# Another order of issue for a kernel of attention and two expert blocks

## The chip, the cores and the metric

The kernel runs on one core of one Trainium2 chip. The metric is the time of one execution on the device in microseconds (us); below it the span is the time from the first to the last instruction of the profiled execution. TensorE is called PE in the rows, VectorE DVE, ScalarE ACT, GpSimd POOL and SyncE SP.

## The reference

Shapes: q, k, v are 4 x 12 x 448 x 64 (batch, head, sequence, dimension); the model width is 768.

```python
q_n, k_n = rmsnorm(q, g_q), rmsnorm(k, g_k)
attn = softmax(q_n @ k_n.T / 8)                 # rows divided by sum + 1e-9
x = (attn @ v), heads joined                    # 4 x 448 x 768

h = relu(x @ w_in)                              # moe: 768 -> 1024
u, v = h[..., :512], h[..., 512:]
v_n = (v - mean) / sqrt(var + 1e-6)
v_s = einsum('ts,bsd->btd', w_spatial, v_n) + b_spatial
x = (u * v_s) @ w_out                           # 512 -> 768

xn = (x - mean) / sqrt(var + 1e-6) * g_ln       # moe2
out = x + relu(xn @ w_ch1) @ w_ch2              # 768 -> 3072 -> 768
```

## The kernel before, in words

All products are taken in fp16 with a high and a low half (a value x becomes fp16(x) and fp16(x - fp16(x))), so a product is three matmuls. A copy on ACT makes the high half, a subtraction on VectorE the low half.

The program has three stages. **Attention** works on 24 pairs of heads. `att_load` fetches q, k (tile `raw`) and v (`vraw`); `att_front` takes squares on ACT (L179) and their sums on VectorE (L180); `att_back` multiplies by the inverse norm (L200), writes the high half on ACT (L202) and the low half (L203, on VectorE for pair 0 and on GpSimd for the others), transposes by DMA (L206) and copies the k halves to the other partitions by two more DMAs (L208). `s_mm` makes scores (L240), `softmax1` takes the negative maximum (L251) and the exp (L256), and `av_mm` multiplies by v. `v_scale` reduces v for its scale: for batch 0 on VectorE (L145), for the others as squares with a sum on ACT (L143). Weights come in a wide format and are unpacked by three VectorE instructions each (L419, L420, L421).

**moe1** runs once for each of four batches and is merged with the attention of the next ones. Its banks are `psv`, `psu`, `pss` and `pso`: L590 makes the v half, L612 the u half (its maximum is taken by L616), L630 and L632 the spatial product (`pss`), which L634 multiplies into u as soon as the scale from the maxima is there, L635 and L636 split the result, and L649 and L659 are the output product, stored to `x2d` in DRAM.

**ffn** is the second expert block. `layernorm` loads `x2d` (`lv`), takes statistics (L680, L681), splits (L695 on ACT, L693 on VectorE), makes the sums of a fast 2 x 2 product (L701 to L704), and transposes by DMA (L697) into `xnT`. It works on half 0 (batches 0 and 1) and half 1. `prep_w1` brings in weights of one of twelve blocks (L535 and L536 split them) and `prep_w2` the second weights (L396). `ffn1` makes seven products in four banks ps1x, ps1y, ps1z and ps1w (L728), combines them on VectorE (L735: tq, tu, td, tc, tb) and splits the hidden values (L740, L741, L759, L760); `ffn2` multiplies (L779) and adds into the output (L783). Attention's memory pool is released before the layernorm's is allocated.

The program above is only the list of work. At its end `issue_order` rearranges it: it makes a graph of all instructions with a cost and a latency for each, and `schedule` goes through it, always issuing the instruction that can start first and, at a tie, the one with the smaller priority number. The priorities come from alternating passes backward and forward. `SHAKES` is a table of triples (seed, spread, passes): in each, a seeded generator picks a stretch of the priorities and shakes them by up to the spread, then the passes run. What comes out is one fixed order for each engine's queue, SP's included (SP issues nearly all DMAs), and each engine runs its queue in that order.

Of the kernel before, what the change touches and what calls it, by code (L numbers as in the profile page):

```python
# [795 lines left out]
def weave(a, b):  # L796

    out = [iter(a), iter(b)]
    while out:
        for g in list(out):  # L800
# [10 lines left out]
WINDOW = 3413  # L811


SHAKES = ((0, 0, 6), (1368, 300, 1), (577, 8000, 1), (1518, 3000, 1), (439, 1000, 1), (1820, 40000, 3), (267, 8000,
          1), (505, 300, 3), (827, 8000, 1), (1565, 8000, 3), (426, 20000, 2), (1065, 20000, 1), (1830, 1000, 3),
          (631, 1000, 1), (625, 40000, 2))


def free_size(ap):
# [225 lines left out]
def issue_order(tc):  # L1045
# [3 lines left out]
    prio = [float(o.n) for o in g.ops]  # L1049
    for seed, spread, passes in SHAKES:  # L1050
        rnd = random.Random(seed)
# [203 lines left out]
```

## Time and profile before

| | us |
|---|---|
| median of 3 runs | 1148.35 |
| lowest, highest | 1147.45, 1148.98 |
| the profiled execution's own time | 1147.53 |
| its span | 1145.7 |
| TensorE busy (93% of the span) | 1060.9 |
| VectorE busy (81%) | 930.2 |
| ACT busy (51%) | 585.3 |
| GpSimd busy (23%) | 267.0 |

A row of a timeline gives an instruction's start and duration; in square brackets behind it stands how long its engine sat idle before it and which instruction or DMA ended that. Busy time is where an engine has an instruction at work; an engine that is busy over the whole of a stretch sets that stretch's length. The granted clock is TensorE's, 1.00 being 2.4 GHz.

### The profile page before, as it was taken

What the parts mean: (1) busy time and instruction counts of PE and PEld (TensorE: products, weight loads), DVE (VectorE), ACT (ScalarE), POOL (GpSimd) and SP (SyncE); (2) the same over time, 40 slices, a digit from 0 to 9 for tenths busy, and PEclk for the clock granted to TensorE, in tenths of its full rate; (3) what the DMA queues carried; (4) which work ended last, traced back from release to release, by engine and by line L of the source; (5) the groups of instructions that cost most, each with busy time, mean ns of one, the idle gap of its engine ahead of it and who ended that gap; (6) DMA issues with size and microseconds to landing.
All of it is one profiled execution on the core that took longest, in us unless ns stands there. A gap on an engine that the chain in (4) does not pass through costs nothing.

```text
span 1145.7 us, 16730 instructions
## 1 busy us (share of the span) xinstructions
PE 1060.9 (93%) x6256; PEld 553.8 (48%) x6256; DVE 930.2 (81%) x1629; ACT 585.3 (51%) x1134; POOL 267.0 (23%) x187
## 2 busy tenths in 40 slices
PE   0699999899999999987799999999999999999998
PEld 0344344444444545343455555555555555555554
DVE  7899999859986987979978878686888888686445
ACT  2799987778876855556332414243243334142110
POOL 3462564366345211113010101011011011010000
PEclk9999999999999999998899999999999999999999
DMA  7988899789898976779752220211122221200013
GB/s 222 275 222 221 181 195 175 154 225 191 155 195 187 186 165 190 149 181 243 151 163 88 78 84 28 83 55 57 57 81 84 83 68 49 78 28 1 1 42 152
DMA packets 229457, 149.56 MB, mean 131 GB/s; under 512 B 190272, under 2 KB 206592, under 8 KB 229376
## 3 DMA queue, kind: packets, MB, share of 16 engines
q1 hardware_dynamic: 224992, 137.49, 50.3%
q10 hardware_dynamic: 4384, 11.01, 3.1%
q8 instruction: 49, 0.80, 0.3%
q14 instruction: 32, 0.26, 0.1%
HBM read 86.30 MB, written 11.01 MB: 85 GB/s over the span
## 4 chain that ended last, share of the span: by engine, by line
PE 50%; DVE 4%; POOL 0%; issue 0%; ACT 0%; DVEq 0%
PE ps L779 27%; PE ps1x L728 6%; PE ps1z L728 6%; PE ps1w L728 6%; PE ps1y L728 3%; DVE x L783 1%; DVE x L693 1%; DVE w1v L536 0%; POOL rsr_x L566 0%; DVE lst L680 0%; DVE r_f L420 0%; ACT x L695 0%; DVE h L741 0%; DVE lv L704 0%; DVE lv L703 0%
## 5 line engine op out<-in xcount | busy, mean ns | idle before, releaser
L779 PE MATMUL ps<-w,h 128*128 128x384 f16 x2016 | 388.1, 330 | 10.8 <-ACT h L740 3.8
L779 PEld LDWEIGHTS <-h 128*128 128x128 f16 x2016 | 198.4, 99 | 161.0 <-issue 13.2
L783 DVE SCALAR_TENSOR_TENSOR x<-ps,wio,x 128x768 f32<-128x768 f32 x168 | 169.6, 1014 | 82.9 <-PE ps L779 81.7
L728 PEld LDWEIGHTS <-w1v 128*128 128x128 f16 x1512 | 147.4, 98 | 129.0 <-issue 5.7
L240 PE MATMUL ps_s<-hT 128*64 128x448 f16 x672 | 102.5, 374 | 41.7 <-DMA hT<-qk 28.5
L256 ACT ACTIVATE pexp<-ps_s,nb 128x448 f32<-128x448 f32 x168 | 108.4, 666 | 29.3 <-DVE nb L251 26.6
L527 POOL TENSOR_TENSOR sums<-r_f 128x384 f32<-128x384 f32 x12 | 14.4, 1199 | 427.7 <-ACT r_f L524 340.5
L728 PE MATMUL ps1x<-xnT,w1v 128*128 128x448 f16 x432 | 110.0, 353 | 0.0
L728 PE MATMUL ps1w<-xnT,w1v 128*128 128x448 f16 x432 | 105.8, 352 | 0.0
L728 PE MATMUL ps1z<-xnT,w1v 128*128 128x448 f16 x432 | 104.6, 352 | 0.0
L251 DVE TENSOR_REDUCE nb<-ps_s 128x2 f32<-128x896 f32 x96 | 91.5, 963 | 12.9 <-PE ps_s L240 12.5
L240 PEld LDWEIGHTS <-hT 128*64 128x64 f16 x672 | 39.0, 111 | 89.3 <-issue 42.0
L203 POOL TENSOR_TENSOR qk<-raw,qk 128x896 f16<-128x896 f32 x23 | 47.4, 2062 | 85.5 <-ACT qk L202 58.9
L590 PE MATMUL psv<-w_v,xT 128*128 128x512 f16 (+1 forms) x360 | 63.1, 343 | 2.5 <-ACT vr L594 2.5
L276 DVE SCALAR_TENSOR_TENSOR p<-pexp,p 128x896 f16<-128x896 f32 (+1 forms) x60 | 64.2, 1071 | 1.4 <-ACT p L275 1.0
L740 ACT ACTIVATE h<-td 128x448 f16<-128x448 f32 x24 | 13.8, 576 | 96.7 <-DVE td L735 96.6
L612 PE MATMUL psu<-xT,w_u 128*128 128x448 f16 x288 | 61.7, 354 | 0.3 <-ACT u L615 0.2
L185 POOL TENSOR_TENSOR rs<-ss,mhalf 128x28 f32<-128x28 f32 (+1 forms) x12 | 57.7, 4810 | 15.0 <-DVE ss L182 7.1
L728 PE MATMUL ps1y<-xnT,w1v 128*128 128x448 f16 x216 | 55.1, 353 | 2.8 <-DMA xnT<-x 2.8
L275 ACT ACTIVATE p<-pexp 128x896 f16<-128x896 f32 (+1 forms) x60 | 51.5, 873 | 1.0 <-DMA pT<-p 0.8
L649 PE MATMUL pso<-w_o,g 128*128 128x384 f16 x288 | 51.3, 327 | 0.7 <-DVE u L634 0.7
L748 ACT ACTIVATE tp<-ps1x 128x448 f32<-128x448 f32 x24 | 12.9, 538 | 76.0 <-PE ps1x L728 76.0
(229 smaller groups left out, 1724.6 us busy)
## 6 DMA issues: line engine op xcount, KB each, us to landing
r_w<-in_moe_w_ch_dram SPq DMA_DIRECT2D x48, 768.0 KB, 4.4
raw<-in_q_dram SPq DMA_DIRECT2D x24, 224.0 KB, 3.9
raw<-in_k_dram SPq DMA_DIRECT2D x24, 224.0 KB, 4.2
vpre<-in_v_dram SPq DMA_DIRECT2D x12, 448.0 KB, 4.6
vraw<-in_v_dram SPq DMA_DIRECT2D x24, 224.0 KB, 4.4
hT<-hT SPq DMA_DIRECT2D x48, 112.0 KB, 3.2
lv<-x2d SPq DMA_DIRECT2D x16, 336.0 KB, 5.1
x<-x2d ACTq DMA_DIRECT2D x14, 384.0 KB, 4.6
```

Source lines behind the costliest of these rows:

```text
L185: nc.gpsimd.tensor_tensor(rs, ss, c.mhalf[:, 0:14 * m], op=ALU.pow)
L240: nc.tensor.matmul(ps[hd * 64:hd * 64 + 64, :S], p.hT[:, blk, hd * 64:hd * 64 + 64], kt[:, :, hd * 64:hd * 64 + 64], start=(t == 0), stop= ...
L251: nc.vector.tensor_reduce(nb[:, 0:n], ps[:, 0:n, :S], axis=AX.X, op=ALU.max, negate=True)
L256: nc.scalar.activation(pe[:, j, :], ps[:, j, :S], AF.Exp, bias=nb[:, j:j + 1], scale=1.0, accum_out=p.sm[:, blk:blk + 1])
L275: nc.scalar.activation(p16[:, 0:n, 0], x, AF.Copy, scale=2.0 ** 14)
L276: nc.vector.scalar_tensor_tensor(p16[:, 0:n, 1], x, 2.0 ** 14, p16[:, 0:n, 0], op0=ALU.mult, op1=ALU.subtract)
L590: nc.tensor.matmul(ps[m * h:m * h + m, 0:hn], xT[:, k, x, t * P:t * P + m], wv[:, w, k, h * hn:(h + 1) * hn], start=(n == 0), stop=(n == l ...
L612: nc.tensor.matmul(ps[:, :S], wu[:, w, k, f * P:(f + 1) * P], xT[:, k, x, :], start=(n == 0), stop=(n == len(mms) - 1))
L649: nc.tensor.matmul(ps[:, 0:384], g16[:, f, g, s0:s0 + m], wo[:, w, f, e * 384:(e + 1) * 384], start=(n == 0), stop=(n == len(mms) - 1))
L728: nc.tensor.matmul(ps, w[:, a, x, d], xnT[:, :, 21 * y + 3 * b + d], start=first and n == 0, stop=n == 8, skip_group_check=True)
L779: nc.tensor.matmul(ps[:, e, 0:QK], h16[:, f, x, t * P:(t + 1) * P], w2[:, y, f, e * QK:(e + 1) * QK], start=n == 0, stop=n == 5)
L783: nc.vector.scalar_tensor_tensor(x2, ps[:, :, 0:QK], io[:, 0:1], x2, op0=ALU.mult, op1=ALU.add)
```

## The change

The table `SHAKES` is replaced by another of the same length. Nothing else differs: the same instructions, in another order on every engine. In the words of the change, the order was picked by its mean time when replayed with shaken durations and clock phases.

```diff
-SHAKES = ((0, 0, 6), (1368, 300, 1), (577, 8000, 1), (1518, 3000, 1), (439, 1000, 1), (1820, 40000, 3), (267, 8000,
...
+SHAKES = ((0, 0, 2), (217, 40000, 1), (1364, 300, 1), (1883, 20000, 1), (170, 20000, 1), (261, 8000, 3), (807, 8000,
...
```

What this moves is shown at three places. Behind an arrow stand the operands, then the size.

**The start, VectorE.** This is the end of the operand for pair 0 (raw_111 is its q and k, qk_0 the fp16 result; v_w and v_f are a raw and an unpacked weight, vpre a part of v, raw_165 pair 1). Before:

```order
L200 TENSOR_TENSOR raw_111<-raw_111,rs_143 128x896
L419 TENSOR_SCALAR v_f<-v_w_290 128x512
L420 SCALAR_TENSOR_TENSOR v_f<-v_w_290,v_f 128x512
L203 TENSOR_TENSOR qk_0_158<-raw_111,qk_0_158 128x14x64
L421 SCALAR_TENSOR_TENSOR v_f<-v_w_290,v_f 128x512
```

Now:

```order
L421 SCALAR_TENSOR_TENSOR v_f<-v_w_290,v_f 128x512
L145 TENSOR_REDUCE vparts_190<-vpre_0_191 128x1
L189 TENSOR_SCALAR rs_143<-rs_143,qa 128x7
L200 TENSOR_TENSOR raw_111<-raw_111,rs_143 128x896
L145 TENSOR_REDUCE vparts_190<-vpre_1_194 128x1
L200 TENSOR_TENSOR raw_165<-raw_165,rs_187 128x896
L203 TENSOR_TENSOR qk_0_158<-raw_111,qk_0_158 128x14x64
```

L421, two L145 and the L200 of pair 1 stand ahead of L203 now. On ACT, the last L143 and the L179 of pair 3 stand ahead of the first L256 instead of behind it, and on SP the two copies L208 of pair 0 follow each other.

**The crossing from moe1 of batch 3 to ffn, VectorE and SP.** On VectorE, the rows from the split of the first `pss` bank to that of the last (u is the gated value, g its fp16 halves, lmv and x_0 belong to the layernorm of half 0, w1v, r_0 and r_1 to weights). Before:

```order
L636 TENSOR_TENSOR g_3_5584<-u_5397,g_3_5584 128x448
L634 SCALAR_TENSOR_TENSOR u_5397<-pss_1_5601,isp_5582,u_5397 128x448
L683 TENSOR_SCALAR lmv_3_0_5504<-lmv_3_0_5504,rsr_x_3_0_5510 112x1
L683 TENSOR_SCALAR lmv_3_1_5516<-lmv_3_1_5516,rsr_x_3_1_5522 112x1
L522 TENSOR_SCALAR wgs_5138<-gln,wsc_0_5135 128x6
L621 TENSOR_TENSOR io_5580<-wsc_g_5577,wsc_o 128x1
L636 TENSOR_TENSOR g_3_5584<-u_5397,g_3_5584 128x448
L634 SCALAR_TENSOR_TENSOR u_5397<-pss_2_5617,isp_5582,u_5397 128x448
L636 TENSOR_TENSOR g_3_5584<-u_5397,g_3_5584 128x448
L634 SCALAR_TENSOR_TENSOR u_5397<-pss_3_5644,isp_5582,u_5397 128x448
```

Now, from two rows behind the first L634 to the row ahead of the last:

```order
L536 TENSOR_TENSOR w1v_5113<-r_0_f,w1v_5113 128x384 x2
L621 TENSOR_TENSOR io_5580<-wsc_g_5577,wsc_o 128x1
L536 TENSOR_TENSOR w1v_5113<-sums_5125,w1v_5113 128x384
L693 TENSOR_TENSOR x_0_2_3_1_5456<-lv_2_5418,x_0_2_3_0_5453 112x1536
L636 TENSOR_TENSOR g_3_5584<-u_5397,g_3_5584 128x448
L634 SCALAR_TENSOR_TENSOR u_5397<-pss_1_5601,isp_5582,u_5397 128x448
L419 TENSOR_SCALAR r_1_f<-r_1_w_5927 128x768
L536 TENSOR_TENSOR w1v_5113<-sums_5125,w1v_5113 128x384
L636 TENSOR_TENSOR g_3_5584<-u_5397,g_3_5584 128x448
L634 SCALAR_TENSOR_TENSOR u_5397<-pss_2_5617,isp_5582,u_5397 128x448
L420 SCALAR_TENSOR_TENSOR r_1_f<-r_1_w_5927,r_1_f 128x768
L636 TENSOR_TENSOR g_3_5584<-u_5397,g_3_5584 128x448
```

The splits of the first ffn1 weight (L536) and the unpacking of the next (L419, L420) have moved ahead of the last L634. In the same stretch on SP, the transposes of the last tile of half 0 (xnT, from x_0_3) and what stands around them. Before:

```order
L697 DMA_TRANSPOSE xnT_5091<-x_0_3_0_0_5526 128x9x112
L697 DMA_TRANSPOSE xnT_5091<-x_0_3_0_1_5529 128x9x112
L697 DMA_TRANSPOSE xnT_5091<-x_0_3_3_0_5536 128x12x112
L697 DMA_TRANSPOSE xnT_5091<-x_0_3_3_1_5539 128x12x112
L676 DMA lv_0_6006<-x2d 112x768 x2
L415 DMA r_1_w_5932<-in_moe_w_ch_dram 128x3x512
L676 DMA lv_1_6131<-x2d 112x768 x2
```

Now:

```order
L697 DMA_TRANSPOSE xnT_5091<-x_0_3_0_0_5526 128x9x112
L697 DMA_TRANSPOSE xnT_5091<-x_0_3_0_1_5529 128x9x112
L415 DMA r_1_w_5932<-in_moe_w_ch_dram 128x3x512
L697 DMA_TRANSPOSE xnT_5091<-x_0_3_3_0_5536 128x12x112
L697 DMA_TRANSPOSE xnT_5091<-x_0_3_3_1_5539 128x12x112
L676 DMA lv_0_6006<-x2d 112x768 x2
L676 DMA lv_1_6131<-x2d 112x768 x2
```

The second load of the next weight (L415, r_1_w) stands ahead of the last two transposes. On TensorE, 15 of the last 24 output matmuls of moe1 stood between ffn1's first ones and now stand ahead of all of them.

**The last wait of the crossing, VectorE.** The combination of ffn1's second block for half 0 (tc, tb, td and ta are its parts, h_1_0 the hidden values that ffn2 multiplies). Before:

```order
L735 SCALAR_TENSOR_TENSOR tc_0_6300<-ps1w_0_6221,tq_0_6209 128x448
L735 SCALAR_TENSOR_TENSOR tb_0_6313<-ps1z_0_6211,tq_0_6209 128x448
L683 TENSOR_SCALAR lmv_3_1_6374<-lmv_3_1_6374,rsr_x_3_1_6380 112x1
L741 SCALAR_TENSOR_TENSOR h_1_0_6186<-td_0_6274,h_1_0_6186 128x448
L693 TENSOR_TENSOR x_1_2_3_1_6269<-lv_2_6231,x_1_2_3_0_6266 112x1536
L760 TENSOR_TENSOR h_1_0_6186<-ta_0_6287,h_1_0_6186 128x448
L741 SCALAR_TENSOR_TENSOR h_1_0_6186<-tc_0_6300,h_1_0_6186 128x448
```

Now:

```order
L735 SCALAR_TENSOR_TENSOR tc_0_6300<-ps1w_0_6221,tq_0_6209 128x448
L735 SCALAR_TENSOR_TENSOR tb_0_6313<-ps1z_0_6211,tq_0_6209 128x448
L683 TENSOR_SCALAR lmv_3_1_6374<-lmv_3_1_6374,rsr_x_3_1_6380 112x1
L741 SCALAR_TENSOR_TENSOR h_1_0_6186<-td_0_6274,h_1_0_6186 128x448
L760 TENSOR_TENSOR h_1_0_6186<-ta_0_6287,h_1_0_6186 128x448
L693 TENSOR_TENSOR x_1_2_3_1_6269<-lv_2_6231,x_1_2_3_0_6266 112x1536
L741 SCALAR_TENSOR_TENSOR h_1_0_6186<-tc_0_6300,h_1_0_6186 128x448
```

L760 stands ahead of the L693 of 1536 columns instead of behind it.

## Rows read from the trace of the kernel before

**Rows 1.** Windows by stage: length, busy time (count) by engine, granted clock, DMA share, GB/s.
```profile
0.00:37.00 37.00, 1.29 (x8) 0.40 (x8) 27.23 (x76) 10.64 (x15) 12.75 (x12) 1.00 0.80 243
...
50.00:222.00 172.00, 154.87 (x959) 72.16 (x953) 164.30 (x294) 156.08 (x343) 84.83 (x47) 0.97 0.89 194
...
222.00:464.00 242.00, 238.14 (x1519) 113.10 (x1519) 200.49 (x360) 173.10 (x343) 97.58 (x67) 1.00 0.88 185
...
464.00:576.00 112.00, 91.55 (x467) 45.42 (x466) 100.96 (x197) 59.52 (x88) 20.81 (x18) 0.91 0.84 184
...
576.00:1145.70 569.70, 564.44 (x3257) 316.89 (x3255) 426.29 (x679) 174.40 (x322) 44.31 (x40) 1.00 0.20 67
```

**Rows 2.** Timeline of the start, VectorE then TensorE: start, us, instruction, [idle <-releaser].
```profile
22.77 1.08 DVE L203 TENSOR_TENSOR qk<-raw,qk 128x896 f16<-128x896 f32 x1
...
23.77 0.69 DVE L421 SCALAR_TENSOR_TENSOR v_f<-v_w,v_f 128x512 int32<-128x512 int32 x1
...
24.71 1.08 DVE L145 TENSOR_REDUCE vparts<-vpre 128x1 f32<-128x896 f32 x1
...
26.84 1.09 DVE L200 TENSOR_TENSOR raw<-raw,rs 128x896 f32<-128x896 f32 x1 [0.45 <-POOL rs L189]
...
28.51 0.96 PE L240 MATMUL ps_s<-hT 128*64 128x448 f16 x4 [28.51 <-DMA hT<-qk]
...
36.99 2.45 PE L240 MATMUL ps_s<-hT 128*64 128x448 f16 x12 [3.89 <-DMA hT<-hT]
```

**Rows 3.** Timeline of the start, ACT.
```profile
40.95 0.94 ACT L143 ACTIVATE vpre<-vpre 128x896 f32<-128x896 f32 x1
...
41.79 0.19 ACT L143 ACTIVATION_READ_ACCUMULATOR vpre<-vpre 128x1 f32 x1
...
42.50 0.94 ACT L179 ACTIVATE sq<-raw 128x896 f32<-128x896 f32 x1
```

**Rows 4.** Timeline of the crossing, TensorE.
```profile
476.28 3.96 PE L630 MATMUL pss<-w_sp,vn 128*128 128x448 f16 x11 [2.09 <-DVE u L634]
...
480.49 2.46 PE L630 MATMUL pss<-w_sp,vn 128*128 128x448 f16 x11
...
487.33 8.63 PE L649 MATMUL pso<-w_o,g 128*128 128x384 f16 x52
...
497.69 0.35 PE L728 MATMUL ps1y<-xnT,w1v 128*128 128x448 f16 x1 [1.72 <-DMA xnT<-x]
...
498.44 1.68 PE L728 MATMUL ps1x<-xnT,w1v 128*128 128x448 f16 x8
...
502.09 1.30 PE L728 MATMUL ps1y<-xnT,w1v 128*128 128x448 f16 x6 [1.08 <-DMA xnT<-x]
...
557.37 0.66 PE L779 MATMUL ps<-w,h 128*128 128x384 f16 x3 [3.82 <-ACT h L740]
...
559.76 14.19 PE L779 MATMUL ps<-w,h 128*128 128x384 f16 x68 [1.73 <-DVE h L760]
```

**Rows 5.** Timeline of the crossing, VectorE.
```profile
483.10 0.62 DVE L636 TENSOR_TENSOR g<-u,g 128x448 f16<-128x448 f32 x1 [1.06 <-ACT g L635]
...
503.50 0.62 DVE L735 SCALAR_TENSOR_TENSOR tq<-ps1y,tp 128x448 f32<-128x448 f32 x1 [4.46 <-PE ps1y L728]
...
557.41 1.75 DVE L693 TENSOR_TENSOR x<-lv,x 112x1536 f16<-112x1536 f32 x1
```

**Rows 6.** Groups by line and form, VectorE: count, busy us, mean ns, idle before.
```profile
L420 DVE SCALAR_TENSOR_TENSOR r_f<-r_w,r_f 128x768 int32<-128x768 int32 x48 | 46.5, 970 | 0.6
...
L419 DVE TENSOR_SCALAR r_f<-r_w 128x768 int32<-128x768 int32 x48 | 27.0, 563 | 0.7 <-DMA r_w<-in_moe_w_ch_dram 0.6
...
L536 DVE TENSOR_TENSOR w1v<-sums,w1v 128x384 f16<-128x384 f32 x48 | 25.6, 550 | 0.0
...
L536 DVE TENSOR_TENSOR w1v<-r_f,w1v 128x384 f16<-128x384 f32 x36 | 24.2, 700 | 3.4 <-ACT w1v L535 3.4
```

**Rows 7.** DMA issues of the page: count, KB each, us to landing.
```profile
r_w<-in_moe_w_ch_dram SPq DMA_DIRECT2D x48, 768.0 KB, 4.4
```

More of the change, by code (lines that the diff above doesn't have):

```diff
@@ L811 @@
 WINDOW = 3413
-SHAKES = ((0, 0, 6), (1368, 300, 1), (577, 8000, 1), (1518, 3000, 1), (439, 1000, 1), (1820, 40000, 3), (267, 8000,
-          1), (505, 300, 3), (827, 8000, 1), (1565, 8000, 3), (426, 20000, 2), (1065, 20000, 1), (1830, 1000, 3),
-          (631, 1000, 1), (625, 40000, 2))
+SHAKES = ((0, 0, 2), (217, 40000, 1), (1364, 300, 1), (1883, 20000, 1), (170, 20000, 1), (261, 8000, 3), (807, 8000,
+          1), (1830, 3000, 1), (1997, 20000, 1), (1777, 1000, 3), (236, 1000, 1), (443, 1000, 1), (172, 8000, 1),
+          (742, 40000, 1), (331, 3000, 2))
 def free_size(ap):
```

## The prediction

> **What bounds the kernel now.** First the windows by stage [rows 1]: the reader is to compare TensorE's busy time with each stretch's length. From 222 to 464 us it is busy 238.1 of 242 us, from 576 to the end 564.4 of 569.7, and what is missing there is the end after the last matmul. Those 812 us hold the same matmuls in any order, so an order can neither shorten nor lengthen them by much. What it can change are three other stretches: the start, 37.0 us with 1.3 us of matmul; attention with the weights of the first expert block, 172.0 us with 154.9, a gap of 17.1; and the crossing from the first block (moe1 of batch 3) to the second (layernorm, ffn1, ffn2), 112.0 us with 91.6, a gap of 20.4. Next the timeline of the start [rows 2]: TensorE waits 28.5 us for the first transposed q and k, then 3.9 us for the copy of the k halves, and VectorE's own queue makes that date, since the subtraction L203 that ends the operand stands behind weight unpacking. Then ACT around the first exp [rows 3], since ACT is busy 156.1 of 172.0 us in the attention stretch and so sets its pace. Last the crossing, on TensorE [rows 4] and on VectorE [rows 5]: TensorE waits 2.1 us inside pss, 1.7 and 1.1 us for transposes, and 3.8 and 1.7 us ahead of ffn2's second block, while VectorE has 101.0 of 112.0 us to do [rows 1]. There VectorE, not TensorE, sets the date.
>
> **The change, part by part.** No instruction is added or removed; every engine's queue is rearranged. So each term is what now stands ahead of the instruction that somebody waits for, priced by the rows of before.
>
> *Start.* Ahead of L203 of pair 0, VectorE's queue gains four instructions: one L421 (0.69), two L145 (1.08 each) and one L200 (1.09) [rows 2]. That is 3.9 us; SP's transpose behind it goes out later by that much, less what VectorE idles today while it waits for weights, for which I take 0.9 (it sat idle 9.8 of the first 37 us [rows 1]): 3.0. The second wait shrinks, because today a weight load goes out between the first copy and the second, and in the new order the two copies stand together. The trace does not price that. Between nothing and the whole 3.0 I take 1.3, nearer to the low end, because the wait of 8.5 us from the first to the second score group (28.51 to 36.99 [rows 2]) is mostly that congestion. So the first exp comes 1.3 us later, bounds 0 and 3.0.
>
> *What ACT has done by then.* In the new order L143 with its readout (0.94 and 0.19) and one L179 (0.94) [rows 3] stand ahead of the first exp instead of behind it: 2.1 us of work that ACT no longer owes in the stretch where it is the busiest. Start and this together: 1.3 - 2.1 = -0.8 us, bounds -2.1 and +0.9.
>
> *Attention.* I counted the instructions ahead of the first and last score block of all 24 pairs. On ACT the count moves by -7 to +6 and on VectorE by -13 to +20, with no trend; at the last exp of pair 9 ACT's count is unchanged, and at the first scores of pairs 11, 12 and 13 TensorE's is the same to the matmul. I take 0. The ends are worked out in the rivals.
>
> *Crossing, the gate of batch 3.* Between the last L616 and the last L634 VectorE now runs five L536 (three from the raw weight, 0.70, and two from sums, 0.55), one L419 (0.56) and one L420 (0.97) [rows 6] that stood behind L634 before: 3 x 0.70 + 2 x 0.55 + 0.56 + 0.97 = 4.7 us. Of that, 1.1 us falls into VectorE's wait for ACT at 483.10 [rows 5], so L634, and with it pss and pso on TensorE, comes 3.6 us later (bounds: 4.7, and nothing if ACT, which idles 52 of 112 us here [rows 1], and the small waits hide it). TensorE then does 15 pso matmuls ahead of ffn1 that stood inside it before: 52 took 8.63 [rows 4], so 15 take 2.5. Its two waits of 1.7 and 1.1 us for transposes are covered by these delays. ffn1's first bank, ps1y, is now complete after 18 matmuls in one piece: eight L728 took 1.68 [rows 4], so 18 take 3.8. Today pso's long piece ends at 495.96 (487.33 + 8.63) and VectorE's tq starts at 503.50 [rows 5]. New: 495.96 + 3.6 + 2.5 + 3.8 = 505.9, which is 2.4 us later.
>
> *Crossing, up to ffn2's second block.* From tq on VectorE has the same work ahead up to tc of the next block (the instructions that pass each other there cancel). Then comes the gain: L760, for which TensorE waits at 559.76, no longer stands behind the L693 of 1.75 us [rows 5]. 2.4 - 1.75 = +0.6 us, bounds -1.7 (tq not later at all) and +1.7 (the gate's 4.7 us in full). Behind that TensorE runs through, and the rest of the program has the same matmuls. The end is the same, with twelve matmuls to each of the last output tiles.
>
> **Sum.** -0.8 + 0 + 0.6 = -0.2 us. The profiled execution itself took 1147.53, with a span of 1145.7; that gives 1147.3. The median of the three runs, 1148.35, is 0.8 above the profiled one, and since a median is to be forecast I add it: **1148.1 us**. What a measurement of this kernel can tell from no change is 0.2%, 2.3 us, so this is no change.
>
> **The clock, row against rule.** Of TensorE's slow matmuls the rows show this: eleven L630 took 3.96 us right behind a wait of 2.1 us, and the same eleven on the next bank, without a wait, 2.46; behind the waits of 3.8 and 1.7 us 68 L779 took 14.19, where 52 pso of the same shape had taken 8.63, so 68 would have taken 11.3 [rows 4]. The granted clock of the crossing averages 0.91 [rows 1], which is some of it at 1.2 GHz and the rest at 2.4. The Trainium skill's page "TensorE: Matmul & The Clock Gate", section "HAM oscillation — how this bites in real kernels", says that work that comes behind a wait starts at the lower clock and that this penalty is paid in addition to the wait; the rows agree. By that rule every wait that the order removes would give time back twice. I do not add it, because up to 559.76 VectorE sets the date and faster matmuls only wait longer; only the 2.9 us of the 68 lie on the path.
>
> **Rivals.**
> - *Attention ends earlier.* At the first reduction of pair 9 VectorE has 13 instructions fewer ahead, and at the last of pair 23 five fewer. At that stretch's mean of 164.3/294 = 0.56 us [rows 1] this is 7.3 and 2.8 us. If the layernorm, which waits for attention's memory, starts 2.8 us earlier and the crossing moves with it, the time is 1148.1 - 2.8 = 1145.3, at the far end 1140.8. Against it: from 222 to 464 us TensorE is full, and a lead of VectorE only waits there.
> - *The half-rate piece goes.* If L760 is ready as TensorE arrives, the 68 matmuls run at full rate: 1148.1 - 2.9 = 1145.2. Against it: the wait of 3.8 us ahead of them is on ACT's h, whose release does not move forward.
> - *Slower: the last transposes queue behind a weight.* On SP the second half of ffn1's next weight, L415, 768 KB, 4.4 us from issue to landing [rows 7], now goes out ahead of the last two transposes of half 0 instead of behind them and the first lv. Its buffer comes free at an L421 that is itself behind the delayed gate. If it holds the transposes up by its whole 4.4 us, ps1y and tq wait for them: 1148.1 + 4.4 = 1152.5. It decides as soon as TensorE's wait before ps1y's last six matmuls is over 1.1 us, as it is today. For it: that wait exists today. Against it: TensorE arrives 2 us later.
>
> **How the numbers follow.** The forecast, within 2.3 us of no change, gets 0.37. Faster gets 0.35: 0.20 for the earlier attention, 0.15 for the half rate. Slower gets 0.28: 0.18 for the transposes, 0.10 for a start with its full 3.0 us and for attention orders such as pair 14's, with eleven more VectorE instructions ahead. The range goes from the first rival's far end, 1140.8, to the third with the start's whole delay on top, 1152.5 + 0.9 + 0.8 = 1154.2, and since the orders of attention can go the other way by the 2.8 us of the first rival, at 1157.0.
>
> **What would show it.** In the new profile: the first score matmul near 31.5 us and the third group of them near 38; ACT busy without a gap from there; tq of block 0 some 2.4 us later than 503.5, with L634 ahead of it 3 to 4 later; the wait on L760 gone or short; from then on TensorE busy to the end. I am wrong if TensorE's gap in the attention stretch is off 17 us by more than 3, if the date of ffn2's second block moves by more than 3, or if waits appear behind 576 us, where there are none now.

## The result, and the profile after

The changed kernel takes **1158.93 us** (median of 4 runs, 1156.69 to 1162.28) against 1148.66 of the kernel before in the same comparison (1147.45 to 1151.22): a ratio of 1.0102, 95% interval 1.0082 to 1.0122. It is slower by 1%, and outside the range of the forecast. The profiled execution took 1158.35 with a span of 1156.6, 10.9 us longer than that of before.

The windows of the changed kernel, first as in [rows 1]. Columns: stretch, length, busy time and count by engine (PE, PE's weight loads, DVE, ACT, POOL), granted clock, DMA share, GB/s.

```profile
0.00:37.00 37.00, 1.31 (x6) 0.47 (x6) 27.26 (x74) 11.57 (x17) 11.42 (x12) 1.00 0.72 218
50.00:222.00 172.00, 152.05 (x955) 71.27 (x955) 167.47 (x301) 156.51 (x343) 87.46 (x47) 0.99 0.90 193
222.00:464.00 242.00, 233.26 (x1462) 106.09 (x1462) 195.11 (x335) 167.16 (x336) 96.52 (x63) 0.99 0.89 185
464.00:576.00 112.00, 89.83 (x467) 43.74 (x462) 102.28 (x213) 64.87 (x94) 23.05 (x22) 0.91 0.72 181
```

The surprise is the third row. TensorE is still busy 233.26 of 242 us, but it has begun only 1462 matmuls, where it began 1519 before [rows 1]. Windows cut at fixed dates can't say more, since the same work no longer lies in the same window. So I number TensorE's matmul records (6256 in both traces) and compare when the n-th one starts; between two of them, the time is split into gaps, in which TensorE has no matmul at work, and work. Between two of the marks below both kernels do the same matmuls, but for at most five of any line. Worked out from the starts and idle times of the timelines, in us:

```
                    start of matmul              between them: time = gaps + work
             1st 1019th 1383rd 1900th 2536th 3100th | 1019-1383      1383-1900        1900-2536       2536-3100
before      28.5  222.0  279.9  364.9  464.0  594.0 | 57.9= 0+57.9   85.0= 2.6+82.4   99.1=1.2+97.9  130.0=20.5+109.6
changed     33.0  222.6  280.0  375.2  474.4  605.4 | 57.4=1.3+56.1  95.2= 6.2+89.0   99.2=1.2+98.0  131.0=22.9+108.1
```

By 222 us, and still by 280 us, the late start is made up: 0.6 and 0.1 us behind. The crossing adds 1.0 us. The whole loss, 10.2 us, arises between the 1383rd and the 1900th matmul, some 290 to 360 us: 3.6 us of gaps, and 6.6 us of work that takes longer. Where a text below speaks of the lag, it is this: how much later than in the kernel before the same work is done.

TensorE's groups by line and form in that stretch show the same matmuls at different prices (count, busy us, mean ns of one, idle before). Before, 290 to 350 us:

```profile
L630 PE MATMUL pss<-w_sp,vn 128*128 128x448 f16 x40 | 9.4, 354 | 0.1
...
L659 PE MATMUL pso<-w_o,g 128*64 128x384 f16 x24 | 3.0, 329 | 0.0
L293 PE MATMUL ps_o<-pT,vraw 128*64 128x448 f32 x12 | 2.6, 539 | 0.0
```

After, 291 to 361 us:

```profile
L630 PE MATMUL pss<-w_sp,vn 128*128 128x448 f16 x40 | 12.2, 413 | 1.0 <-DVE vn L604 0.6 <-ACT pT L271 0.4
...
L659 PE MATMUL pso<-w_o,g 128*64 128x384 f16 x24 | 4.6, 340 | 0.0
L293 PE MATMUL ps_o<-pT,vraw 128*64 128x448 f32 x12 | 3.6, 548 | 0.0
```

The same 40, 24 and 12 matmuls are 5.4 us dearer. A mean of one hardly moves for L659 (329 and 340 ns), but their sum grows by half: a row's time includes the overlap with its neighbours, and it is the neighbours that changed.

Three places account for it. First, TensorE's timeline at the gate of batch 1 (start, us, instruction, [idle <-releaser]). After:

```profile
309.51 0.95 PE L240 MATMUL ps_s<-hT 128*64 128x448 f16 x8 [0.46 <-ACT pexp L256]
312.59 0.24 PE L83 MATMUL pssc_g<-ssb_g,ones 128*128 128x1 bf16 x4 [2.13 <-DVE ssb_g L80]
313.38 2.65 PE L630 MATMUL pss<-w_sp,vn 128*128 128x448 f16 x6 [0.56 <-DVE vn L604]
...
318.19 2.56 PE L630 MATMUL pss<-w_sp,vn 128*128 128x448 f16 x8
```

Before, at the same place:

```profile
305.74 0.24 PE L83 MATMUL pssc_g<-ssb_g,ones 128*128 128x1 bf16 x4 [0.51 <-DVE sst_V L87]
...
306.79 2.46 PE L630 MATMUL pss<-w_sp,vn 128*128 128x448 f16 x11
```

A wait of 2.13 us, then one of 0.56, and behind them six L630 take 2.65 and eight 2.56 us, where eleven took 2.46: matmuls at the lower of the two clocks (1.2 GHz). The granted clock averages 0.95 from 291 to 361 us after, and 1.00 from 290 to 350 us before.

Second, what VectorE and GpSimd do ahead of that wait (after, VectorE's queue, then GpSimd's):

```profile
307.95 1.85 DVE L308 TENSOR_SCALAR sm<-sm 128x7 f32<-128x7 f32 x1
309.71 0.15 DVE L618 TENSOR_TENSOR gm<-gm 128x4 f32<-128x4 f32 x1
309.78 1.08 DVE L276 SCALAR_TENSOR_TENSOR p<-pexp,p 128x896 f16<-128x896 f32 x1
310.78 0.19 DVE L309 RECIPROCAL sm<-sm 128x7 f32<-128x7 f32 x1
310.89 1.03 DVE L251 TENSOR_REDUCE nb<-ps_s 128x2 f32<-128x896 f32 x1
311.85 0.61 DVE L331 TENSOR_TENSOR xo<-ps_o,rb 128x448 f32<-128x448 f32 x1
312.38 0.15 DVE L80 CAST ssb_g<-gm 128x4 bf16<-128x4 f32 x1
```

```profile
307.58 2.18 POOL L203 TENSOR_TENSOR qk<-raw,qk 128x896 f16<-128x896 f32 x1 [3.65 <-ACT qk L202]
```

The cast L80 that TensorE waits for stands behind four instructions, and ahead of those the tiny L308, which takes 0.16 us in the median of its 24 instances, takes 1.85: it ends when GpSimd's product ends. Third, TensorE from 340 us, where the L659 of batch 1 stand in pieces:

```profile
340.57 0.36 PE L630 MATMUL pss<-w_sp,vn 128*128 128x448 f16 x1
340.87 0.35 PE L659 MATMUL pso<-w_o,g 128*64 128x384 f16 x1
341.15 0.93 PE L630 MATMUL pss<-w_sp,vn 128*128 128x448 f16 x4
342.01 0.35 PE L659 MATMUL pso<-w_o,g 128*64 128x384 f16 x2
```

Before, most of them stand in one piece:

```profile
337.04 1.47 PE L659 MATMUL pso<-w_o,g 128*64 128x384 f16 x16
```

In the changed kernel there is no gap here and no wait, and TensorE is busy throughout; yet a lone L659 holds it from 340.87 to 341.15, 0.28 us, where before sixteen together took 1.47.

### The profile page after: what moved, and what is told of

It reads as the page before. It is cut to its first block, busy times and chain, and to the rows that moved or that the text cites. A ratio compares the mean times of both kernels' runs of the same rounds, so it can differ in the third digit from the quotient of the medians.

```text
span 1156.6 us, 16718 instructions
## 1 busy us (share of the span) xinstructions
PE 1061.0 (92%) x6256; PEld 549.8 (48%) x6256; DVE 938.9 (81%) x1629; ACT 586.7 (51%) x1134; POOL 268.5 (23%) x187
## 4 chain that ended last, share of the span: by engine, by line
PE 48%; DVE 2%; ACT 0%; issue 0%; ACTq 0%
PE ps L779 26%; PE ps1w L728 6%; PE ps1z L728 6%; PE ps1x L728 6%; PE ps1y L728 3%; DVE x L783 1%; DVE x L693 0%; DVE r_f L420 0%; DVE h L741 0%; ACT r_f L524 0%; DVE r_f L421 0%; DVE w1v L536 0%; DVE td L735 0%; ACT h L740 0%; DVE tu L735 0%
## 5 line engine op out<-in xcount | busy, mean ns | idle before, releaser
L779 PE MATMUL ps<-w,h 128*128 128x384 f16 x2016 | 367.4, 329 | 13.2 <-ACT h L740 7.1
L256 ACT ACTIVATE pexp<-ps_s,nb 128x448 f32<-128x448 f32 x168 | 107.3, 653 | 27.2 <-DVE nb L251 23.9
L240 PE MATMUL ps_s<-hT 128*64 128x448 f16 x672 | 104.6, 370 | 17.7 <-ACT pexp L256 12.9
L251 DVE TENSOR_REDUCE nb<-ps_s 128x2 f32<-128x896 f32 x96 | 91.7, 963 | 13.3 <-PE ps_s L240 13.3
L728 PE MATMUL ps1w<-xnT,w1v 128*128 128x448 f16 x432 | 96.9, 352 | 2.5 <-DVE wsc L89 2.1
L728 PE MATMUL ps1x<-xnT,w1v 128*128 128x448 f16 x432 | 98.2, 352 | 0.6 <-DVE tc L735 0.5
L728 PE MATMUL ps1z<-xnT,w1v 128*128 128x448 f16 x432 | 96.8, 352 | 1.4 <-DVE td L735 1.4
L240 PEld LDWEIGHTS <-hT 128*64 128x64 f16 x672 | 39.6, 110 | 94.7 <-issue 43.4
L203 POOL TENSOR_TENSOR qk<-raw,qk 128x896 f16<-128x896 f32 x23 | 49.1, 2134 | 71.2 <-ACT qk L202 71.2
L185 POOL TENSOR_TENSOR rs<-ss,mhalf 128x28 f32<-128x28 f32 (+1 forms) x12 | 60.9, 5076 | 13.5 <-DVE ss L182 12.2
L612 PE MATMUL psu<-xT,w_u 128*128 128x448 f16 x288 | 62.8, 354 | 1.2 <-ACT vr L594 1.2
L276 DVE SCALAR_TENSOR_TENSOR p<-pexp,p 128x896 f16<-128x896 f32 (+1 forms) x60 | 57.7, 964 | 3.2 <-ACT p L275 3.1
L649 PE MATMUL pso<-w_o,g 128*128 128x384 f16 x288 | 51.4, 327 | 2.2 <-ACT g L635 1.3
L630 PE MATMUL pss<-w_sp,vn 128*128 128x448 f16 (+1 forms) x176 | 47.0, 382 | 4.7 <-DVE u L634 3.8
L270 PE MATMUL ps_t<-ident,pexp 128*128 128x128 f32 x252 | 44.1, 297 | 7.8 <-ACT pT L271 4.3
```

The costliest lines, as they stand in the source:

```text
L185: nc.gpsimd.tensor_tensor(rs, ss, c.mhalf[:, 0:14 * m], op=ALU.pow)
L240: nc.tensor.matmul(ps[hd * 64:hd * 64 + 64, :S], p.hT[:, blk, hd * 64:hd * 64 + 64], kt[:, :, hd * 64:hd * 64 + 64], start=(t == 0), stop= ...
L251: nc.vector.tensor_reduce(nb[:, 0:n], ps[:, 0:n, :S], axis=AX.X, op=ALU.max, negate=True)
L256: nc.scalar.activation(pe[:, j, :], ps[:, j, :S], AF.Exp, bias=nb[:, j:j + 1], scale=1.0, accum_out=p.sm[:, blk:blk + 1])
L276: nc.vector.scalar_tensor_tensor(p16[:, 0:n, 1], x, 2.0 ** 14, p16[:, 0:n, 0], op0=ALU.mult, op1=ALU.subtract)
L612: nc.tensor.matmul(ps[:, :S], wu[:, w, k, f * P:(f + 1) * P], xT[:, k, x, :], start=(n == 0), stop=(n == len(mms) - 1))
```

## The experiments

**Which stretch: six cuts.** Every queue follows one order up to a matmul of TensorE and the other from there. The planner is run with both tables, and its list of all instructions in the order in which it issued them (`settle`) is cut; the edit is the same for all, and only `PARTS` differs (a number counts TensorE's instructions, 72 fewer than the trace's records at these places):

```diff
+    lines = {s: settle(g, s) for s in (OLD, NEW)}
+    line, put = [], set()
+    for table, until in PARTS:
+        count = 0
+        for o in lines[table]:
+            count += o.eng == "PE"
+            if until and count > until:
+                break
+            if o.n not in put:
+                line.append(o)
+                put.add(o.n)
...
-    for l in schedule(g, prio)[1].values():
+    for l in order.values():
         for a, b in zip(l, l[1:]):
```

`PARTS = ((NEW, 1311), (OLD, 0))`:

> Every queue follows the new order up to the 1383rd matmul that the trace records (280 us in both profiles) and the old order from there. Theory M (the 10 us are lost between 290 and 350 us, in the stretch that the prediction took for full): the time of before, 1147 to 1151 us. Theory S (the start and the first 280 us of the new order cost it, and the late lead only shows it): 1156 to 1160 us. Theory C (the crossing to the second expert block costs it): 1147 to 1151 us, as with M.

`PARTS = ((OLD, 1311), (NEW, 1750), (OLD, 0))`:

> Old order up to the 1383rd recorded matmul (280 us), new order from there to the 1822nd (350 us in before, 361 in after), old order behind it. Theory M: slower than before by 8 to 11 us, 1156 to 1160 us, with TensorE waiting some 2 us for the gate's scale ssb_g near 310 us and a spell of half clock behind it. Theories S and C: 1147 to 1151 us. If the loss needs the state that the new order had built up by 280 us, it comes out between.

`PARTS = ((OLD, 2464), (NEW, 0))`:

> Old order up to the 2536th recorded matmul (464 us in before), new order from there: the crossing and all behind it are new. Theory M: the crossing by itself is worth about what the lead shows there, from 10.6 us at 460 to 11.4 at 600: 1148 to 1151 us, no change. Theory C: 1156 to 1160 us. A third outcome, faster than before by 2 to 4 us, would say that the new crossing is the better one and that its arrival 10 us late hid it.

Measured: 1150.21 (ratio to before 1.0023, 1.0008 to 1.0037), 1158.57 (1.0107, 1.0089 to 1.0125) and 1153.00 us (1.0060, 1.0041 to 1.0079). The middle alone costs what the whole change costs. But the first and the third cost something too, and the three sum to more than the whole. In the first run's trace the lag rises by 3.4 us within 5 us of the seam, and in the third's by 7 within 20 us: where one order takes over from another at a place at which the engines stand differently far, the seam seems to have a price. So the cuts were made again where both orders stand equal.

`PARTS = ((NEW, 947), (OLD, 0))`:

> New order up to the 1019th recorded matmul (222 us in both profiles, where the lead of the old order had shrunk to 0.9 us), old order from there. The run that changed over at 280 us lost 3.3 us; its lag on TensorE rose only behind the seam, from 1 to 4.4 us between 280 and 290 us. Theory M (start and attention cost under 1 us, that loss is the seam's): 1147 to 1149 us, within 0.2% of before. Theory S (work that the new order had left undone by 280 us): slower than before by 3 us or more.

`PARTS = ((OLD, 947), (NEW, 2255), (OLD, 0))`:

> Old order up to the 1019th recorded matmul (222 us), new order to the 2327th (430 us in before, 440 in after, inside a stretch where the lag is flat), old order behind it: the seams lie where both orders stand equal. Theory M: 1156 to 1159 us, with a lag of 8 to 10.5 us at 360 us, of which some 3 us are added gaps, 3 us half clock behind the wait for the gate, and the rest matmuls that take longer because half-array ones no longer stand together. Theory C: 1147 to 1150 us.

`PARTS = ((OLD, 2255), (NEW, 0))`:

> Old order up to the 2327th recorded matmul (430 us in before), new order from there: the crossing again, with the seam 34 us earlier than in the run that lost 6.1 us, whose first waits (4.2 us on ACT's u) came within 10 us of its seam. If the new crossing by itself is that dear: 1151 to 1154 us. If it was the seam: 1147 to 1150 us, since the changed kernel's lag went only from 10.6 to 11.4 us over the same stretch.

Measured: start and attention 1147.63 us (1.0003, 0.9990 to 1.0015), the middle 1158.93 (1.0104, 1.0085 to 1.0124), the crossing 1148.99 (1.0014, 1.0002 to 1.0027). Theory M holds and S and C fall: the stretch from 222 to 430 us carries the loss. In the middle run the matmuls 1383 to 1900 took 97.5 us, 8.0 of gaps and 89.5 of work, close to the changed kernel's 95.2. The crossing, cut 34 us earlier, costs 5 us less than in the first cut, which fits a price of the seam.

**VectorE beside GpSimd.** One instruction moved behind three:

```diff
+    move(order["DVE"], r"vr1_3_\d+", 0, 3)
```

> The new order with one instruction of VectorE moved: the product L600 of the last piece of batch 1 (3.49 us at 289.5 us, beside two products of GpSimd, where the same shape took 0.54 in before) goes behind the two reductions L616 and the reduction L251 that follow it. Theory P (VectorE stands still while GpSimd multiplies, and these 2.9 us reach TensorE through the gate's scale): L600 takes 0.5 to 0.6 us, the wait for ssb_g shrinks from 2.1 us to under 0.5, and 3 to 6 us come back: 1153 to 1156 us. Theory Q (the place of the gate's scale L80 behind four instructions sets its date, the stall only fills slack): under 1 us comes back, 1157 to 1160 us.

1156.70 us (1.0097, 1.0078 to 1.0116), against 1.0102 for the changed kernel: no gain that can be told. L600 took 0.53 us instead of 3.49, as meant, but VectorE then sat idle 1.44 us for ACT's u, and at the gate the trace shows the same wait of 2.13 us and the same L308 of 1.85. The time lies between the two theories' ranges; by the rows this stall lay in slack, as theory Q has it.

**The gate.**

```diff
+    behind(order["DVE"], r"gm2_1_\d+", 0, r"nb17_0_\d+", 0)
+    behind(order["DVE"], r"ssb_g1_\d+", 0, r"p16_16_1_\d+", 0)
+    behind(order["DVE"], r"vn16_1_\d+", -1, r"p16_15_2_\d+", 0)
```

> The new order with three instructions of VectorE's queue moved ahead by 2 to 25 places at 294 to 307 us: the sum L618 and the cast L80 of batch 1's gate go right behind the last reduction L616, and the last product L604 of that batch goes to where its input is ready. Theory G (TensorE's wait of 2.1 us for ssb_g, 0.6 us for vn, and the sixteen matmuls at half clock behind them, some 2.9 us, come from these places): all three go, 1152.5 to 1155.5 us. Theory R (the loop scores, maximum, exp, transposes sets the pace of that stretch, and TensorE would wait elsewhere): under 1.5 us back, 1157 to 1160 us.

1155.01 us (1.0076, 1.0058 to 1.0095): 2.6 thousandths, 3.0 us, of the changed kernel's loss come back, which is Theory G's size. But the difference of the two ratios is uncertain by some 3 us, and in the profile the matmuls 1383 to 1900 take 93.4 us instead of 95.2, 1.8 less. TensorE's rows of this run:

```profile
309.43 0.25 PE L83 MATMUL pssc_g<-ssb_g,ones 128*128 128x1 bf16 x4
309.54 1.51 PE L630 MATMUL pss<-w_sp,vn 128*128 128x448 f16 x6
312.46 0.57 PE L240 MATMUL ps_s<-hT 128*64 128x448 f16 x4 [1.41 <-ACT pexp L256]
```

Both waits are gone, and six L630 take 1.51 us instead of 2.65; the granted clock from 290 to 354 us is 1.00. Work between matmuls 1383 and 1900 falls from 89.0 to 86.6 us. The gaps grow from 6.2 to 6.8, since waits for exp (4.8 us there, 2.6 in the changed kernel) take the place of those for the gate, as Theory R has it for the waits. Behind the largest of them, 1.41 us, stands VectorE's row

```profile
306.99 1.85 DVE L80 CAST ssb_g<-gm 128x4 bf16<-128x4 f32 x1
```

Now the cast stands where L308 stood, and takes 1.85 us in its place: what stalls is whatever VectorE does as GpSimd's product starts.

**The gate, and the product out of the way.**

```diff
+    behind(order["Activation"], r"qk16_19_\d+", 0, r"pexp17_1_\d+", -1)
```

> The earlier gate once more, and on ACT's queue the cast L202 of pair 19 behind the next two exps (7 instructions later), which lets GpSimd's product L203 of that pair start some 7 us later. In the run with the earlier gate alone VectorE's cast L80 took 1.85 us instead of 0.15 beside that product, and TensorE then waited 1.4 us for an exp. Theory P (VectorE stands still while GpSimd multiplies, and in this stretch that reaches TensorE): the stall of 1.7 us and the wait of 1.4 us go, another 1 to 2.5 us back, 1152.5 to 1154.5 us. Theory Q (the stall fills slack): as the earlier gate alone, 1154.5 to 1156 us.

1154.57 us (1.0055, 1.0042 to 1.0069); beside 1.0076, another 2.1 thousandths, 2.4 us. The intervals of the two overlap and 1154.57 lies on the border of the two theories, so the time alone does not decide; the rows do. In the profile the matmuls 1383 to 1900 take 91.4 us, 2.0 less than with the earlier gate alone. VectorE and GpSimd:

```profile
305.91 0.16 DVE L80 CAST ssb_g<-gm 128x4 bf16<-128x4 f32 x1
305.99 0.16 DVE L308 TENSOR_SCALAR sm<-sm 128x7 f32<-128x7 f32 x1
...
310.60 1.61 DVE L251 TENSOR_REDUCE nb<-ps_s 128x2 f32<-128x896 f32 x2
```

```profile
310.56 1.89 POOL L203 TENSOR_TENSOR qk<-raw,qk 128x896 f16<-128x896 f32 x1 [8.72 <-ACT qk L202]
```

The stall is gone, and so is TensorE's wait of 1.41 us. The product now runs beside L251, two reductions out of a bank, which take 1.61 us as they do anywhere. By the rows Theory P holds here, where Q held for L600: the same kind of stall is free in one place, and in another about its whole length reaches TensorE.

**The widths.**

```diff
+    together(order["PE"], r"pso1_3_\d+", r"pso1_3_\d+", r"pso1_4_0_\d+", r"pso1_3_\d+")
```

> The new order with TensorE's queue alone rearranged between 340 and 356 us: the 24 L659 of batch 1, which write half of the array's columns and stand there in pieces of 1 to 6 among full-width L630, L649 and L293, are put together in one piece. In the trace of the changed kernel an L612 behind an L612 starts 189 ns after it, but an L240 behind an L612 285 ns after it, and the same 285 the other way: each change between half and full width costs some 96 ns. This order has 14 such changes fewer (350 instead of 364). Theory W (changes of width are part of the loss): 1.3 us back in the lag at 360 us, time 1156.5 to 1158.5 us. Theory N (TensorE only waits less or more there): no change, 1157.5 to 1160 us, lag as before.

1155.37 us (1.0070, 1.0051 to 1.0089): 3.2 thousandths, 3.7 us, come back, more than twice what was expected. (Counted in the traces' records, the widths change 336 times in the changed kernel, 322 times here and 325 times in the kernel before; the totals given with this and the following expectations are some 25 to 35 higher, which leaves the 14 of this edit and the 18 of the next as they are.) TensorE:

```profile
341.65 3.38 PE L293 MATMUL ps_o<-pT,vraw 128*64 128x448 f32 x16
344.96 2.14 PE L659 MATMUL pso<-w_o,g 128*64 128x384 f16 x24
```

From the L300 at 338 us on, the same matmuls as in the changed kernel take 3.2 us less, of which 14 changes at 96 ns are 1.3. The other part, as far as the starts show it: two half-width matmuls on different halves of the array start within 30 ns of each other and run together, and pieces of odd length leave one alone. Of the 24 L659 and 16 L293, 26 held TensorE for a time of their own in the changed kernel and 20 here; three L659 of 0.16 us and three L293 of 0.37 are 1.6 us. Beyond these 3.2 us, the 3.7 is uncertain by some 3 us, and this profile had less of the low clock at the gate (0.98 from 290 to 375 us, 0.96 in the changed kernel), which the edit does not touch.

Two counts keep this in proportion. From the 1019th to the 2536th matmul the two orders change width equally often, 179 times before and 178 in the changed kernel; but up to the 1383rd the changed order has 16 fewer (43 instead of 59), and there its work is 1.8 us shorter, and from there to the 1900th it has 16 more (81 instead of 65). And the 40 L659 and L293 together hold TensorE 6.6 us before, 8.2 in the changed kernel and 5.4 in this run, worked out from the starts: the edit takes away more than the change had added.

The other way round, in the old order:

```diff
+    for b in range(3):
+        mix(order["PE"], rf"pso{b}_3_\d+", rf"pso{b}_4_0_\d+")
```

> The same price measured the other way: the old order, with 24 L659 and 12 L649 of each of batches 0 to 2 put in turns of two and one on TensorE's queue, 18 changes of width more (368 instead of 350), all in stretches where TensorE is full. Theory W: 18 x 96 ns = 1.7 us more lag, built up near 245, 335 to 345 and 435 us, and 1148 to 1150 us. Theory N: the time of before, 1146 to 1148 us, and no lag. If new waits for g appear at these places, they come on top and are told apart by their rows.

1150.86 us (1.0023, 1.0013 to 1.0033), 2.6 us slower. All 18 changes fell into batch 1, since in batches 0 and 2 no tile bears the second name. The lag between 330 and 352 us rises by 3.1 us: 0.9 of two new waits (L634, L662), 2.2 of longer work, 0.12 us a change. TensorE there:

```profile
343.22 0.35 PE L659 MATMUL pso<-w_o,g 128*64 128x384 f16 x2
343.51 0.34 PE L649 MATMUL pso<-w_o,g 128*128 128x384 f16 x1
343.77 0.35 PE L659 MATMUL pso<-w_o,g 128*64 128x384 f16 x2
344.06 0.34 PE L649 MATMUL pso<-w_o,g 128*128 128x384 f16 x1
```

From one pair of L659 to the next, with one L649 between, it takes 0.55 us; in pieces of their own, a pair took 0.18 (24 in 2.14 us, above) and an L649 0.16, together 0.34. Theory W holds in both directions, with a price somewhat above 96 ns.

**All four edits** of the changed order, in one kernel: L600, the gate, the product and the widths.

> The new order with all four edits: the earlier gate, the later cast L202, the 24 L659 together, and the later L600. If the costs add up: 3 us for the gate, 1 to 2.5 for the product, 1.3 for the widths, 0.5 for L600, so 1150.5 to 1152.5 us, which is 4 to 6 above before. If they hide one another (one loop sets the pace and takes up each gain): 1153.5 to 1156 us.

1150.41 us (1.0024, 1.0013 to 1.0034). The single gains are 0.5, 2.6, 2.1 and 3.2 thousandths, 8.4 together; 7.8 came back of 10.2. They add up, within the noise. The matmuls 1383 to 1900 take 86.7 us (3.6 of gaps, 83.1 of work), 1.7 more than before.

**The old order with fewer changes of width.** If the price is real, the kernel before pays it 325 times.

```diff
+    for k, o in enumerate(left[:reach + 1]):
+        if half(o) == half(out[-1]) and not any(passed.get(a.n, 0) >= reach or needs(o, a) for a in left[:k]):
+            break
```

> The old order with TensorE's queue gathered by width between 222 and 464 us: where the next matmul writes another width of the array (half or all columns) than the one before, one of the same width is taken from among the three behind it, if nothing it needs stands between; no matmul is passed by more than three. That leaves 295 changes of width of 350, so 55 fewer. Theory W at 96 ns a change: 5.3 us less, 1141 to 1144 us, faster than before and than the changed kernel, with the lag falling in steps between 222 and 464 us, the crossing giving part of it back (an order that came early there has waited before). Theory N: no gain, 1146 to 1149 us. If matmuls taken ahead are not ready, waits of 0.2 to 1 us appear on TensorE in that stretch and eat it up.

> The same with a reach of six: 266 changes of width, 84 fewer than the old order. Theory W: 8.1 us less by 464 us, 1139 to 1143 us with what the crossing gives back. Theory N: 1146 to 1149 us. With this reach a matmul waits up to 1.2 us longer for its turn, so new waits for exp and for transposes are likelier than with three; if they win, it comes out between the run with three and before.

With a reach of three **1145.22 us** (0.9973, 0.9960 to 0.9987), faster than before and than the changed kernel, between the ranges of the two theories. With six 1149.89 (1.0021, 1.0007 to 1.0034), slower than before. From 222 to 464 us, worked out as above, with the changes of width counted in the records:

```
                         changes      time = gaps + work (us, matmul 1019 to 2536)
before                       179     242.0 =  3.9 + 238.1
reach 3                      118     240.6 =  9.7 + 230.8
reach 6                       86     243.0 = 15.4 + 227.7
reach 4, scores stay         125     240.4 =  8.9 + 231.5
reach 8, scores stay         103     243.8 = 12.7 + 231.1
changed kernel               178     251.8 =  8.7 + 243.1
```

The price holds: 61 fewer changes and 7.3 us less work with a reach of three, 0.12 us each, and 0.09 to 0.12 in the other three runs. (Gathering also leaves fewer half-width matmuls without a partner, which is in this price.) The last row shows that the count alone does not make the loss: the changed kernel has as many changes as before. But gaps take most of it back, such as these, reach of three and then of six:

```profile
265.52 0.57 PE L240 MATMUL ps_s<-hT 128*64 128x448 f16 x4 [1.01 <-ACT pexp L256]
```

```profile
314.03 0.57 PE L240 MATMUL ps_s<-hT 128*64 128x448 f16 x4 [1.51 <-ACT pexp L256]
...
412.32 0.76 PE L300 MATMUL ps_o<-pT,v 128*64 128x448 f16 x6 [1.26 <-ACT rb L320]
```

Two more runs asked whether scores issued later made these waits (the rule adds one condition to the one above):

```diff
+        ... or (stay and re.match(stay, wrote(a))) for a in left[:k]):
```

> Gathered as before, with a reach of four, but no matmul for which ACT and VectorE wait in the softmax (scores ps_s, transposes ps_t, the row sums ps_r) is passed by another. 302 changes of width, 48 fewer than the old order. In the run with a reach of three TensorE worked 7.5 us less between 222 and 464 us and waited 5.9 us more, mostly for exp. Theory L (the added waits come from scores and transposes issued later, which holds up the loop of maximum, exp and transposes): work falls by 5 to 6.5 us, waits grow by under 3 us, 1143 to 1145 us. Theory E (TensorE has run into the pace of ACT and VectorE, whatever its order): waits grow by as much as the work falls, 1145 to 1148 us.

> The same with a reach of eight: 284 changes of width, 66 fewer. Theory L: work falls by 7 to 9 us, waits by under 4 us more, 1141 to 1144 us. Theory E: no faster than with a reach of four, 1145 to 1149 us, the longer reach of six without this rule having been slower than before.

1145.22 us (0.9987, 0.9976 to 0.9998) and 1148.32 (1.0011, 1.0003 to 1.0020). Work fell by 6.6 and 7.0 us, and the gaps grew by 5.0 and 8.8 although no score was passed by; most of the growth is waits for exp (0.6 us before, 4.9 and 7.7 here). Theory L falls. Theory E fits: the loop of maximum (VectorE), exp (ACT), product and transposes would set a pace of about 240 us for this stretch, and TensorE, at 238 of 242, would be no more than level with it. That is inferred from where the gains went; no run made ACT or VectorE faster by itself, and matmuls other than scores still changed places. With the long reach something is lost besides; which wait that begins with was not followed up.

## Why the prediction was wrong

*What bounds the kernel.* Here it failed, in the sentence that the 812 us in which TensorE is full "hold the same matmuls in any order, so an order can neither shorten nor lengthen them by much". They hold the same matmuls, but not the same time. Busy time was read as work that can't change; in it lie changes of width, pairs that do or don't overlap, and the clock. The changed order loses 10.2 us in 517 of these matmuls: 3.6 in gaps, and 6.6 in work. Of the work, 2.4 is the low clock behind the gate's waits (what the run with the earlier gate takes away), 1.6 lies in L659 and L293, with their changes of width and lost pairs, 1.5 in L240, though there are four fewer of them, and 1 is spread over the other lines; what made the L240 dearer, no run took apart. The four edits bring back 7.8 thousandths, but part of that is that the run with widths made L659 and L293 cheaper than they had been before. And full did not mean bound: the runs with gathered widths suggest that 98% busy is what TensorE shows where it and the loop of maximum, exp and product are level, and in the run with the product out of the way a delay of VectorE of 1.7 us did reach TensorE. From the 1900th matmul to the crossing none of the lag is made up (10.3 and 10.4 us).

*Start.* The first score starts at 33.08 us (31.5 foretold), the large group at 38.95 (38 foretold, 36.99 before, [rows 2]):

```profile
32.98 0.16 PE L83 MATMUL pssc_V<-ssb_V,ones 128*128 128x1 bf16 x1 [32.98 <-DVE ssb_V L80]
33.08 0.59 PE L240 MATMUL ps_s<-hT 128*64 128x448 f16 x2
...
38.95 2.45 PE L240 MATMUL ps_s<-hT 128*64 128x448 f16 x12 [4.65 <-DMA hT<-hT]
```

The first exp goes from 39.49 to 41.44 us, so it is 2.0 us later instead of 1.3, inside the bounds. The first score is 4.6 us later where 3.0 was worked out; the second wait swallowed more of it than foretold. The cut run shows that start and attention together cost 0.3 thousandths (-1.0 to 1.5). The forecast of -0.8 for start and ACT and 0 for attention stands within what is measured, though the changed order runs up to 8 us late between 90 and 200 us on the way, which no count of instructions had shown.

*Crossing.* Right in its dates up to tq. In the run with the new crossing alone, whose lag is -1.1 us where it begins, the last L634 starts at 485.87 us against 483.64, 3.3 us later (3.6 foretold), and tq at 504.53 against 503.50, 2.1 later (2.4 foretold). The wait on L760 is gone. What took its place:

```profile
547.25 3.36 PE L728 MATMUL ps1w<-xnT,w1v 128*128 128x448 f16 x9 [2.10 <-DVE wsc L89]
...
558.99 2.74 PE L779 MATMUL ps<-w,h 128*128 128x384 f16 x8 [6.13 <-ACT h L740]
```

A single wait of 6.13 us for ACT's h, instead of 3.82 and 1.73 [rows 4]: with L760 out of the way, ACT set the date. The crossing costs 1.6 us by itself (1.4 thousandths, 0.2 to 2.7; 0.6 foretold, bounds -1.7 and 1.7). Of the signs of being wrong, the date of ffn2's second block gave it away: in the changed kernel it moved by over 10 us, nearly all of it lost long before. The rival of the transposes queuing behind a weight does not show: the waits for xnT are gone.

*The rivals.* The one on attention was dismissed because TensorE is full from 222 us on; the same reason, turned round, hid the loss. The slower rivals both lay at places that I had already found to wait. None lay where TensorE was full, and the range ended 1.9 us below the result.

*The clock.* That a wait can be paid twice was used for waits that go, and not for waits that might come. At the gate it was half of the matter: 2.7 us of waits and some 2.4 of slow matmuls behind them. The Trainium skill's page "TensorE: Matmul & The Clock Gate", section "HAM oscillation — how this bites in real kernels", describes a kernel in which matmuls behind a wait start at the lower clock and pay for it on top of the wait; the run with the earlier gate agrees, in which both went together.

## What to carry to other kernels

Before a full engine's stretch is called fixed, compare the sum of its rows by form with another order's: "busy" holds changes of width, lost overlap and slow clock as well as work. For each wait in or just ahead of such a stretch, look at what the waiting engine's partners do there, since what was lost there was not made up here. And to find where an order loses time, cut two orders together at places where they stand equal: a cut elsewhere seems to have a price of its own, here some 2 to 5 us.

## What the hardware showed that I had not expected

*A change of width costs TensorE about 0.1 us.* Starts of neighbours without a gap, from 222 to 464 us of the changed kernel, worked out from the trace: in the median, an L612 starts 189 ns behind an L612 (110 times), an L240 behind an L612 283 (14 times) and an L612 behind an L240 285 (18 times); an L649 163 behind an L649, an L659 behind an L649 261. L240 and L659 write 64 columns, the others 128. The Trainium skill's page "TensorEngine Tiling (Array Packing)", section "Key Properties", says that changing the tiling mode, and not just the tile, drains TensorE. The runs agree and give the number, 0.12 us a change when added to the old order and 0.09 to 0.12 when taken from it. A change of the rows alone costs the same: an L630 of 64 rows starts 285 ns behind one of 128 rows (8 times, median), and one of 128 behind another 189. I had not looked for this rule; but it would not have foretold the loss by a count, since the two orders differ by 11 changes in all, some 1 us.

*A product on GpSimd can hold up an instruction on VectorE until it ends.* L308 and L80, 0.15 us each elsewhere, took 1.85 beside it, and it is not only small ones: in the kernel before, two L276 of 896 columns took 2.44 and 2.23 us beside an L203, and 1.08 in the median. Reductions (L251, L616) ran at their usual length. The Trainium skill's page "SBUF — State Buffer", section "Who interferes with whom", says that the two engines share a pair of ports under an exclusive lock and that a reduction does not contend on trn2; the rows agree on both.

*One order has a scatter of several us.* In the profile of the run with more changes of width, whose execution was the longest of its twelve (1154.96 us), 3.8 us were lost near 170 us, far ahead of its edit and at a place where its queues equal before's. A difference of single profiles is worth little without the place where it arises.
